# 64-key remainder of a sigmoid attention in 64 by 64 products, placed behind the full chunks, with its pieces of v loaded for six pairs at once

## The chip, the cores and the metric

The kernel runs on one core of one Trainium2 chip. The core has a matrix engine (PE, with its weight loads shown apart as PEld), a vector engine (DVE), a scalar engine (ACT), GpSimd (POOL) and a queue that only issues transfers (SP), and all of them take their instructions in the order of the program. Products land in PSUM, eight banks of 2 KB for each of 128 partitions; everything else is in SBUF. The metric is the device time of one execution in microseconds; lower is better.

## The reference, cut to what matters

Sigmoid attention over 4 batches, 12 heads, 448 positions and 64 channels a head, then two expert layers on the 1792 tokens of 768 channels, all in float32:

```python
def _attn_ref(q, k, v):                       # (4, 12, 448, 64) each
    S = q.shape[2]
    scale = 1.0 / np.sqrt(q.shape[-1])
    scores = scale * np.matmul(q, k.transpose(0, 1, 3, 2)) - np.log(S)
    attn = 1.0 / (1.0 + np.exp(-scores))
    return np.matmul(attn, v).astype(np.float32)

def reference(**kwargs):
    attn_out = _attn_ref(**attn_kwargs)
    x = np.ascontiguousarray(attn_out.transpose(0, 2, 1, 3)).reshape(B * S, H * D)
    x = _moe_ref(x=x, **moe_kwargs)           # h = x @ w_in; (h - tanh(h)) @ w_out, 2048 wide
    return _moe2_ref(x=x, **moe2_kwargs)      # (sigmoid(x @ w_gate) * (x @ w_val)) @ w_out, 1536 wide
```

The weights of the two layers come to the chip as 64-bit floats and are decoded there.

## The kernel before

The 48 heads are taken as 24 pairs (NP); pair p has heads j = 0 and 1, and six pairs (HPB) make a batch. The 448 keys are cut into NCH = 4 chunks of CP = 112. For each pair:

- `load` (L142) brings k and q, with channels on partitions: head j lies on partitions 64j to 64j+63. Each is two transfers of 64 rows, on SP's queue but for the first q. Three buffers each, so pair p+3 is loaded as soon as `split(p)` has read pair p. `load_v` (L155) brings v of a pair in one transfer, keys on 112 partitions.
- `split` (L162) makes of each k and q a rounded high part and a low part (the rest) in fp32r, the faster format of PE: four DVE instructions. The program calls it one pair ahead, and it issues the loads of the pair three ahead.
- `scores` (L191) takes each chunk's transposed scores, keys on partitions, as three products (high by high, low by high, high by low) for each head; contraction is over 64 channels, so the heads use the two halves of the rows of the array. ACT turns them into attention with a sigmoid, into `at`. The two middle chunks use a tile `pa` of two banks and one activation for both heads, the two outer ones a one-bank tile `pb` for each head and two activations. These shapes are the names `sa` and `sb` in the rows below.
- `values` (L226) multiplies with v in plain fp32 (each such product is two instructions in the trace), keys contracted, head j on the column half j of the array and on partitions 64j of the result `pv`, 448 columns wide. ACT copies the result as the high part of x, and DVE subtracts to get the low part.

The program is in the order written by hand (`manual_schedule`, L373), and every engine follows that order; waits between engines are put in by the framework. In the loop over pairs (L395) the order is scores(p), split(p+1), values(p-1). Between them, from pair 3 on, one step at a time of `decode` (L91) for the first seven weight blocks: a (ACT), b and c (DVE; c also fetches a later block), d (ACT and GpSimd), which takes three pairs for a block; `fetch` (L83) issues the transfer of a block of 768 KB on SP, the first two at p = 2 and p = 4. In the last pair, the first expert product `hidden_mm(0)` (L260) and the head of its activations (`hidden_act`, L270: five on ACT, then steps on DVE) come before the values of pair 22, and values(23) follows behind the loop.

After attention the expert layers run as a chain of 80 steps of `hidden_mm` and `project` (L335), in three fp32r products for each block (`mm3`, L246). PSUM: `psa` has two tiles of two banks, `psb` four of one bank (L68, L69).

Of the kernel before, what the change touches and what calls it, by code (L numbers as in the profile page):

```python
# [32 lines left out]
def kernel(  # L33
# [12 lines left out]
    nc = tc.nc  # L46
# [13 lines left out]
    KR = NCH * 128  # L60
# [8 lines left out]
    psb = ctx.enter_context(tc.tile_pool(name="psb", bufs=4, space=bass.MemoryType.PSUM))  # L69
# [72 lines left out]
    def load(p):  # L142

        if p >= NP:
            return
        kt = qkp.tile([128, S], F32, tag="kt", name=f"kt{p}")
        qt = qkp.tile([128, S], F32, tag="qt", name=f"qt{p}")
        for t, src, by in ((kt, k, nc.sync), (qt, q, nc.sync if p else nc.scalar)):

            for j in (0, 1) if by is nc.sync else (1, 0):  # L150
                r = slice(j * D, (j + 1) * D)
                by.dma_start(out=t[r], in_=src[p, r, j])
        qk_t[p] = (qt, kt)

    def load_v(p):  # L155
        if p >= NP:
            return
        vt = atp.tile([CP, 2, NCH, D], F32, tag="vt", name=f"vt{p}")
        nc.sync.dma_start(out=vt, in_=v[p])
        v_t[p] = vt  # L160

    def split(p):  # L162
# [5 lines left out]
        kk = t[:, :2 * KR].rearrange("p (i c r) -> p i c r", i=2, r=128)[:, :, :, :CP]  # L168
        qq = t[:, 2 * KR + QGAP:].rearrange("p (i s) -> p i s", i=2)
        ks = kt.rearrange("p (c r) -> p c r", r=CP)  # L170
        k0 = kk[:, 0].bitcast(F32)
        q0 = qq[:, 0].bitcast(F32)
        if p:
            nc.vector.tensor_copy(out=kk[:, 0], in_=ks)
            nc.vector.tensor_tensor(out=kk[:, 1], in0=ks, in1=k0, op=ALU.subtract)
            nc.vector.tensor_copy(out=qq[:, 0], in_=qt)
            nc.vector.tensor_tensor(out=qq[:, 1], in0=qt, in1=q0, op=ALU.subtract)
        else:

            nc.scalar.activation(out=qq[:, 0], in_=qt, func=AF.Copy)  # L180
            a, b = slice(0, 1), slice(1, NCH)
            nc.vector.tensor_copy(out=kk[:, 0, a], in_=ks[:, a])
            nc.vector.tensor_tensor(out=kk[:, 1, a], in0=ks[:, a], in1=k0[:, a], op=ALU.subtract)
            nc.vector.tensor_copy(out=kk[:, 0, b], in_=ks[:, b])
            nc.vector.tensor_tensor(out=qq[:, 1], in0=qt, in1=q0, op=ALU.subtract)
            nc.vector.tensor_tensor(out=kk[:, 1, b], in0=ks[:, b], in1=k0[:, b], op=ALU.subtract)
        s_t[p] = kk, qq
        load(p + 3)
        load_v(p + 3)

    def scores(p):  # L191

        kk, qq = s_t.pop(p)
        at = atp.tile([CP, 2, NCH, S], F32, tag="at", name=f"at{p}", bufs=2)
        a_t[p] = at

        for c in range(NCH):
            two = 0 < c < NCH - 1
            if two:
                pa = psa.tile([128, 2, 512], F32, tag="pa", name=f"sa{p}_{c}")  # L200
                o = [pa[:CP, j, :S] for j in range(2)]
            else:
                o = []
                for j in range(2):
                    pb = psb.tile([128, 512], F32, tag="pb", name=f"sb{p}_{c}_{j}")
                    o.append(pb[:CP, :S])
            for i, (ki, qi) in enumerate(((0, 0), (1, 0), (0, 1))):
                for j in range(2):
                    r = slice(j * D, (j + 1) * D)
                    nc.tensor.matmul(  # L210
                        o[j], kk[r, ki, c], qq[r, qi],
                        start=(i == 0), stop=(i == 2),
                    )
            if two:
                nc.scalar.activation(  # L215
                    out=at[:, :, c], in_=pa[:CP, :, :S], func=AF.Sigmoid,
                    bias=bias_s[:CP], scale=qk_scale,
                )
            else:
                for j in range(2):  # L220
                    nc.scalar.activation(  # L221
                        out=at[:, j, c], in_=o[j], func=AF.Sigmoid,
                        bias=bias_s[:CP], scale=qk_scale,
                    )

    def values(p):  # L226
        b, hp = divmod(p, HPB)
        at = a_t.pop(p)
        vt = v_t.pop(p)
        po = psb.tile([128, 512], F32, tag="pb", name=f"pv{p}")  # L230
        for c in range(NCH):
            for j in range(2):
                nc.tensor.matmul(  # L233
                    po[j * D:(j + 1) * D, :S], vt[:, j, c], at[:, j, c],
                    start=(c == 0), stop=(c == NCH - 1),
                )
        xh, xl = x[b][:, 0, hp], x[b][:, 1, hp]
        nc.scalar.activation(out=xh, in_=po[:, :S], func=AF.Copy)
        nc.vector.tensor_tensor(out=xl, in0=po[:, :S], in1=xh.bitcast(F32), op=ALU.subtract)
# [133 lines left out]
    with tc.manual_schedule():  # L373
# [8 lines left out]
        load_v(0)  # L382
        load(2)
        load_v(1)
# [4 lines left out]
        pz = psb.tile([128, 512], F32, tag="pb", name="pz")  # L389
# [5 lines left out]
        for p in range(NP):  # L395
# [10 lines left out]
            if p == NP - 1:  # L406
                qk_ctx.close()
# [10 lines left out]
            if p:  # L418
                values(p - 1)
            if len(todo) in (2, 3):  # L420
                todo.pop(0)()
# [3 lines left out]
        values(NP - 1)  # L425
        att_ctx.close()
        ap_ = ctx.enter_context(tc.tile_pool(name="ap", bufs=NB, reuse_waits="tile"))
# [87 lines left out]
```

## Time and profile before

| | |
|---|---|
| Median of 3 runs | 1132.23 us (1132.17 to 1132.34) |
| Profiled execution | 1133.54 us, its span 1131.7 us |
| PE busy | 1124.8 us (99% of the span), 5869 products |
| PEld busy | 994.1 us (88%) |
| DVE busy | 774.6 us (68%) |
| ACT busy | 461.9 us (41%) |
| POOL busy | 215.2 us (19%) |
| Granted clock of PE | 0.999 of 2.4 GHz |
| DMA | 76.44 MB in 24068 packets, mean 68 GB/s |

The profile is of one execution, from its first to its last instruction; the span is that stretch, and the execution's own time has what lies around it. A page gives busy times of each engine, the chain of work that ended last, and groups of instructions; the trace behind it can be asked for an instruction's start, its length and what it waited for. A PE instruction's length is the time until its result is out, so one that follows the other without a gap still overlaps it; what it costs is the distance of two starts. The clock is near full in every slice. Attention takes the first 154 us, the expert layers the rest.

### The profile page before, as it was taken

How to read it: one execution, taken by the hardware profiler on the slowest of the kernel's cores; microseconds unless marked ns; L12 is line 12 of the kernel's file. 1: busy time of each engine (PE TensorE's matmuls, PEld its weight loads, DVE VectorE, ACT ScalarE, POOL GpSimd, SP SyncE). 2: the span in 40 equal slices, each digit the busy share in tenths (PEclk: the TensorE clock that was granted, in tenths of full speed). 3: DMA queues.
4: the chain of work that ended last, by engine and by line, in shares of the span. 5: the costliest groups of instructions: out<-in, count | busy, mean ns of one | idle time of the engine just before them, and what ended most of it. 6: DMA issues, size and time to landing. Idle time of an engine off the chain costs nothing.

```text
span 1131.7 us, 14544 instructions
## 1 busy us (share of the span) xinstructions
PE 1124.8 (99%) x5869; PEld 994.1 (88%) x5869; DVE 774.6 (68%) x1118; ACT 461.9 (41%) x619; POOL 215.2 (19%) x144
## 2 busy tenths in 40 slices
PE   9999999999999999999999999999999999999998
PEld 5555589999999999999999999999999999999997
DVE  3666556888888888888897755656656655665643
ACT  7888844455554444444454321221212212222110
POOL 0011000111111111111128612312312222222210
PEclk9999999999999999999999999999999999999999
DMA  6655300111111111111110211210211201201014
GB/s 192 178 178 159 105 29 1 56 57 56 56 56 56 56 57 56 55 49 51 52 48 28 84 56 35 78 56 29 84 36 49 84 29 56 80 33 56 28 45 152
DMA packets 24068, 76.44 MB, mean 68 GB/s; under 512 B 3392, under 2 KB 12608, under 8 KB 24000
## 3 DMA queue, kind: packets, MB, share of 16 engines
q1 hardware_dynamic: 23840, 75.28, 20.4%
q8 instruction: 46, 0.75, 0.3%
q10 hardware_dynamic: 160, 0.23, 0.1%
q14 instruction: 22, 0.18, 0.1%
HBM read 69.99 MB, written 5.51 MB: 67 GB/s over the span
## 4 chain that ended last, share of the span: by engine, by line
PE 99%; DVE 1%; ACT 0%; issue 0%; ACTq 0%
PE ph L248 17%; PE ph L247 17%; PE ph L249 17%; PE po L248 12%; PE po L247 12%; PE po L249 12%; PE pv L233 7%; PE sb L210 3%; PE sa L210 3%; DVE acc L349 1%; PE pz L391 0%; ACT at L221 0%; ACT at L215 0%; DVE y L282 0%; DVE z L388 0%
## 5 line engine op out<-in xcount | busy, mean ns | idle before, releaser
L349 DVE TENSOR_TENSOR acc<-po,acc 128x448 f32<-128x448 f32 x432 | 251.5, 616 | 249.3 <-PE po L249 249.3
L247 PE MATMUL ph<-x,w 128*128 128x448 f32 x960 | 348.2, 363 | 0.4 <-ACT at L215 0.4
L248 PE MATMUL ph<-x,w 128*128 128x448 f32 x960 | 348.4, 363 | 0.0
L249 PE MATMUL ph<-x,w 128*128 128x448 f32 x960 | 345.6, 360 | 0.0
L128 POOL TENSOR_TENSOR w<-m,w 128x768 fp32r<-128x768 f32 x68 | 126.0, 1852 | 733.7 <-ACT w L127 721.3
L248 PE MATMUL po<-g,w 128*128 128x448 f32 x672 | 244.0, 363 | 0.0
L247 PE MATMUL po<-g,w 128*128 128x448 f32 x672 | 243.6, 362 | 0.0
L249 PE MATMUL po<-g,w 128*128 128x448 f32 x672 | 241.9, 360 | 0.0
L247 PEld LDWEIGHTS ph<-x,w 128*128 128x128 f32 x960 | 180.2, 188 | 15.4 <-ACT at L215 0.8
L249 PEld LDWEIGHTS ph<-x,w 128*128 128x128 f32 x960 | 179.5, 187 | 12.7
L248 PEld LDWEIGHTS ph<-x,w 128*128 128x128 f32 x960 | 180.2, 188 | 9.5
L279 ACT ACTIVATE sg<-ph 128x448 f32<-128x448 f32 x48 | 26.2, 545 | 337.4 <-PE ph L249 337.4
L247 PEld LDWEIGHTS po<-g,w 128*128 128x128 f32 x672 | 126.2, 188 | 9.8
L249 PEld LDWEIGHTS po<-g,w 128*128 128x128 f32 x672 | 125.7, 187 | 8.9
L248 PEld LDWEIGHTS po<-g,w 128*128 128x128 f32 x672 | 126.1, 188 | 6.9 <-POOL g L284 0.3
L101 ACT ACTIVATE m<-st 128x768 f32<-128x768 f32 x68 | 61.8, 908 | 101.4 <-POOL w L128 100.3
L284 POOL TENSOR_TENSOR g<-y,g 128x448 fp32r<-128x448 f32 x48 | 57.3, 1193 | 166.6 <-ACT g L283 128.5
L300 ACT ACTIVATE u<-ph 128x896 f32<-128x896 f32 x32 | 29.4, 918 | 121.0 <-PE ph L249 121.0
L233 PE MATMUL pv<-at,vt 112*64 112x448 f32 x384 | 77.2, 545 | 0.0
L117 DVE SCALAR_TENSOR_TENSOR m<-st,m 128x768 int32<-128x768 int32 x68 | 67.6, 995 | 2.4
L113 DVE SCALAR_TENSOR_TENSOR m<-st,m 128x768 int32<-128x768 int32 x68 | 67.5, 993 | 1.1
L233 PEld LDWEIGHTS pv<-at,vt 112*64 112x64 f32 x384 | 25.5, 136 | 41.3 <-issue 40.7
(48 smaller groups left out, 967.6 us busy)
## 6 DMA issues: line engine op xcount, KB each, us to landing
st<-in_w_out_dram SPq DMA_DIRECT2D x28, 768.0 KB, 4.4
st<-in_w_in_dram SPq DMA_DIRECT2D x16, 768.0 KB, 4.3
st<-in_w_gate_dram SPq DMA_DIRECT2D x12, 768.0 KB, 4.4
st<-in_w_val_dram SPq DMA_DIRECT2D x12, 768.0 KB, 4.2
kt<-in_k_dram SPq DMA_DIRECT2D x48, 112.0 KB, 3.6
vt<-in_v_dram SPq DMA_DIRECT2D x24, 224.0 KB, 2.8
out_dram<-acc SPq DMA_DIRECT2D x24, 224.0 KB, 2.3
qt<-in_q_dram SPq DMA_DIRECT2D x46, 112.0 KB, 3.2
```

Of the source, the lines that this page charges most:

```text
L101: nc.scalar.activation(out=mf, in_=hi.bitcast(F32), func=AF.Abs)
L113: nc.vector.scalar_tensor_tensor(out=m, in0=hi, scalar=-0x40000000, in1=m, op0=ALU.bitwise_and, op1=ALU.bitwise_or,)
L117: nc.vector.scalar_tensor_tensor(out=m, in0=lo, scalar=29, in1=m, op0=ALU.logical_shift_right, op1=ALU.bitwise_or,)
L128: nc.gpsimd.tensor_tensor(out=w1, in0=mf, in1=w0.bitcast(F32), op=ALU.subtract)
L210: nc.tensor.matmul(o[j], kk[r, ki, c], qq[r, qi], start=(i == 0), stop=(i == 2),)
L233: nc.tensor.matmul(po[j * D:(j + 1) * D, :S], vt[:, j, c], at[:, j, c], start=(c == 0), stop=(c == NCH - 1),)
L247: nc.tensor.matmul(o, wt[(slice(None), 0) + wsl], r[(slice(None), 0) + rsl], start=first, stop=False)
L248: nc.tensor.matmul(o, wt[(slice(None), 0) + wsl], r[(slice(None), 1) + rsl], start=False, stop=False)
L249: nc.tensor.matmul(o, wt[(slice(None), 1) + wsl], r[(slice(None), 0) + rsl], start=False, stop=last)
L284: nc.gpsimd.tensor_tensor(out=gt[:, 1, 0], in0=y, in1=gt[:, 0, 0].bitcast(F32), op=ALU.subtract)
L300: nc.scalar.activation(out=uu, in_=h, func=AF.Square)
L349: nc.vector.tensor_tensor(out=at[:, d], in0=po[:, :S], in1=at[:, d], op=ALU.add)
```

## The change

The keys are now cut in three full chunks of 128 and 64 keys left over (KL). The host still hands over v in four chunks of 112 rows, so the kernel puts the chunks of 128 together: 112 rows from the chunk itself and 16 (EX) from the fourth; the last 64 rows of the fourth are the ones left over.

- Loads: k and q get four buffers. v gets one tile for six pairs (VG), two buffers. A pair's three chunks still come pair by pair (now runs of 768 bytes), and the fourth chunk's rows come as ten small transfers for six pairs at once: for each head two copies of the 64 rows left over (on partitions 0 to 63 and on 64 to 127), and three of 16 rows. All their runs are 256 bytes. Those of the first six pairs are issued five before and five behind `load(2)`, later ones three for each `split`.
- `split` works on k in two parts (112 of each chunk's rows and the 16), and leaves the 64 keys alone.
- `scores` takes three chunks, each into two banks with one activation for both heads. The banks are handed out in turn from `psa` (two tiles) and a new `psx` (one tile `px`).
- `scores_last` takes the 64 keys straight from k and q in plain fp32: for each head and each half of 224 positions (SH), a product of 64 channels by 64 keys, on its own quarter of the array, with one activation of 448 columns for all.
- `values` takes the full chunks in two halves of 224 positions, into `pv`, which has one buffer of two banks. `values_last` adds the 64 keys' part, again one quarter of the array for each head and half, and then come the copy and the subtraction as before.
- The order in a pair is scores(p), split(p+1), values(p-1), scores_last(p), values_last(p-1). In the last pair scores_last comes ahead of `hidden_mm(0)`. `psb` is opened behind attention, in the banks of `psx`.

```diff
--- before.py
+++ after.py
@@ -57,7 +57,11 @@
     N1 = G1 * NB
     N2 = F2 * NB
     NSTEP = N1 + N2
-    KR = NCH * 128
+    KR = (NCH - 1) * 128
+    KL = S - KR
+    EX = 128 - CP
+    VG = HPB
+    SH = S // 2
     qk_scale = 1.0 / math.sqrt(D)
     qk_bias = -math.log(S)
@@ -66,7 +70,9 @@
     stp = ctx.enter_context(tc.tile_pool(name="stp", bufs=2))
     dp = ctx.enter_context(tc.tile_pool(name="dp", bufs=1))
     psa = ctx.enter_context(tc.tile_pool(name="psa", bufs=2, space=bass.MemoryType.PSUM))
-    psb = ctx.enter_context(tc.tile_pool(name="psb", bufs=4, space=bass.MemoryType.PSUM))
+    psx_ctx = ExitStack()
+    psx = psx_ctx.enter_context(tc.tile_pool(name="psx", bufs=1, space=bass.MemoryType.PSUM))
     x = [xp.tile([128, 2, KD, S], F32R, tag=f"x{b}", name=f"x{b}") for b in range(NB)]
@@ -143,8 +149,8 @@
         if p >= NP:
             return
-        kt = qkp.tile([128, S], F32, tag="kt", name=f"kt{p}")
-        qt = qkp.tile([128, S], F32, tag="qt", name=f"qt{p}")
+        kt = qkp.tile([128, S], F32, tag="kt", name=f"kt{p}", bufs=4)
+        qt = qkp.tile([128, S], F32, tag="qt", name=f"qt{p}", bufs=4)
         for t, src, by in ((kt, k, nc.sync), (qt, q, nc.sync if p else nc.scalar)):
             for j in (0, 1) if by is nc.sync else (1, 0):
@@ -153,11 +159,38 @@
         qk_t[p] = (qt, kt)
     def load_v(p):
         if p >= NP:
             return
-        vt = atp.tile([CP, 2, NCH, D], F32, tag="vt", name=f"vt{p}")
-        nc.sync.dma_start(out=vt, in_=v[p])
-        v_t[p] = vt
+        g, n = divmod(p, VG)
+        if n == 0:
+            v_t[g] = atp.tile([128, VG, 2, NCH, D], F32, tag="vt", name=f"vt{g}", bufs=2)
+            rest_of(g)
+        nc.sync.dma_start(out=v_t[g][:CP, n, :, :NCH - 1], in_=v[p, :, :, :NCH - 1])
+    pieces = []
+    def rest_of(g):
+        vt = v_t[g]
+        ps = slice(g * VG, (g + 1) * VG)
+        for j in range(2):
+            for h in range(2):
+                pieces.append((
+                    vt[h * KL:(h + 1) * KL, :, j, NCH - 1],
+                    v[ps, CP - KL:, j, NCH - 1].rearrange("n r d -> r n d"),
+                ))
+            for c in range(NCH - 1):
+                pieces.append((
+                    vt[CP:, :, j, c],
+                    v[ps, c * EX:(c + 1) * EX, j, NCH - 1].rearrange("n r d -> r n d"),
+                ))
+    def load_pieces(n):
+        for _ in range(min(n, len(pieces))):
+            o, i = pieces.pop(0)
+            nc.sync.dma_start(out=o, in_=i)
     def split(p):
@@ -165,78 +198,104 @@
             return
         qt, kt = qk_t.pop(p)
         t = qkp.tile([128, 2 * KR + QGAP + 2 * S], F32R, tag="sp", name=f"sp{p}", bufs=2)
-        kk = t[:, :2 * KR].rearrange("p (i c r) -> p i c r", i=2, r=128)[:, :, :, :CP]
+        kk = t[:, :2 * KR].rearrange("p (i c r) -> p i c r", i=2, r=128)
         qq = t[:, 2 * KR + QGAP:].rearrange("p (i s) -> p i s", i=2)
-        ks = kt.rearrange("p (c r) -> p c r", r=CP)
-        k0 = kk[:, 0].bitcast(F32)
-        q0 = qq[:, 0].bitcast(F32)
+        parts = (
+            (kt[:, :KR - (NCH - 1) * EX].rearrange("p (c r) -> p c r", r=CP), slice(0, CP)),
+            (kt[:, (NCH - 1) * CP:KR].rearrange("p (c r) -> p c r", r=EX), slice(CP, 128)),
+        )
+        for src, r in parts:
+            nc.vector.tensor_copy(out=kk[:, 0, :, r], in_=src)
+        if p == 0:
+            nc.scalar.activation(out=qq[:, 0], in_=qt, func=AF.Copy)
+        for src, r in parts:
+            nc.vector.tensor_tensor(
+                out=kk[:, 1, :, r], in0=src, in1=kk[:, 0, :, r].bitcast(F32), op=ALU.subtract
+            )
         if p:
-            nc.vector.tensor_copy(out=kk[:, 0], in_=ks)
-            nc.vector.tensor_tensor(out=kk[:, 1], in0=ks, in1=k0, op=ALU.subtract)
             nc.vector.tensor_copy(out=qq[:, 0], in_=qt)
-            nc.vector.tensor_tensor(out=qq[:, 1], in0=qt, in1=q0, op=ALU.subtract)
...
+        nc.vector.tensor_tensor(out=qq[:, 1], in0=qt, in1=qq[:, 0].bitcast(F32), op=ALU.subtract)
+        s_t[p] = kk, qq, kt, qt
         load(p + 3)
         load_v(p + 3)
+        load_pieces(3)
+    slots = [0]
+    l_t = {}
+    o_t = {}
+    def slot(name):
+        n = slots[0]
+        slots[0] += 1
+        if n % 3 < 2:
+            return psa.tile([128, 2, 512], F32, tag="pa", name=name)
+        return psx.tile([128, 2, 512], F32, tag="px", name=name)
     def scores(p):
-        kk, qq = s_t.pop(p)
...
+        kk, qq, kt, qt = s_t.pop(p)
+        at = atp.tile([128, 2, NCH - 1, S], F32, tag="at", name=f"at{p}", bufs=2)
+        al = atp.tile([128, 2, SH], F32, tag="al", name=f"al{p}", bufs=2)
+        a_t[p] = at, al
+        l_t[p] = kt, qt, al
+        for c in range(NCH - 1):
+            pa = slot(f"sa{p}_{c}")
+            for i, (ki, qi) in enumerate(((0, 0), (0, 1), (1, 0))):
                 for j in range(2):
                     r = slice(j * D, (j + 1) * D)
                     nc.tensor.matmul(
-                        o[j], kk[r, ki, c], qq[r, qi],
+                        pa[:, j, :S], kk[r, ki, c], qq[r, qi],
                         start=(i == 0), stop=(i == 2),
                     )
-            if two:
-                nc.scalar.activation(
-                    out=at[:, :, c], in_=pa[:CP, :, :S], func=AF.Sigmoid,
-                    bias=bias_s[:CP], scale=qk_scale,
+            nc.scalar.activation(
+                out=at[:, :, c], in_=pa[:, :, :S], func=AF.Sigmoid,
+                bias=bias_s, scale=qk_scale,
+            )
+    def scores_last(p):
+        kt, qt, al = l_t.pop(p)
+        pl = slot(f"sl{p}")
+        for h in range(2):
+            for j in range(2):
+                r = slice(j * D, (j + 1) * D)
+                nc.tensor.matmul(
+                    pl[h * KL:(h + 1) * KL, j, :SH], kt[r, KR:], qt[r, h * SH:(h + 1) * SH],
+                    start=True, stop=True,
                 )
-            else:
+        nc.scalar.activation(
+            out=al, in_=pl[:, :, :SH], func=AF.Sigmoid, bias=bias_s, scale=qk_scale
+        )
+    def values(p):
+        at, al = a_t.pop(p)
+        g, n = divmod(p, VG)
+        vt = v_t[g]
+        po = psx.tile([128, 2, 512], F32, tag="pv", name=f"pv{p}")
+        for h in range(2):
+            for c in range(NCH - 1):
                 for j in range(2):
-                    nc.scalar.activation(
-                        out=at[:, j, c], in_=o[j], func=AF.Sigmoid,
-                        bias=bias_s[:CP], scale=qk_scale,
+                    nc.tensor.matmul(
+                        po[j * D:(j + 1) * D, h, :SH], vt[:, n, j, c],
+                        at[:, j, c, h * SH:(h + 1) * SH],
+                        start=(c == 0), stop=False,
                     )
-    def values(p):
+        o_t[p] = po, al, vt, n
+    def values_last(p):
         b, hp = divmod(p, HPB)
-        at = a_t.pop(p)
-        vt = v_t.pop(p)
-        po = psb.tile([128, 512], F32, tag="pb", name=f"pv{p}")
-        for c in range(NCH):
+        po, al, vt, n = o_t.pop(p)
+        for h in range(2):
+            r = slice(h * KL, (h + 1) * KL)
             for j in range(2):
                 nc.tensor.matmul(
-                    po[j * D:(j + 1) * D, :S], vt[:, j, c], at[:, j, c],
-                    start=(c == 0), stop=(c == NCH - 1),
+                    po[j * D:(j + 1) * D, h, :SH], vt[r, n, j, NCH - 1], al[r, j],
+                    start=False, stop=True,
                 )
-        xh, xl = x[b][:, 0, hp], x[b][:, 1, hp]
-        nc.scalar.activation(out=xh, in_=po[:, :S], func=AF.Copy)
-        nc.vector.tensor_tensor(out=xl, in0=po[:, :S], in1=xh.bitcast(F32), op=ALU.subtract)
+        xh, xl = (x[b][:, i, hp].rearrange("p (h s) -> p h s", h=2) for i in range(2))
+        nc.scalar.activation(out=xh, in_=po[:, :, :SH], func=AF.Copy)
+        nc.vector.tensor_tensor(out=xl, in0=po[:, :, :SH], in1=xh.bitcast(F32), op=ALU.subtract)
     h_t = {}
     g_t = {}
@@ -380,13 +439,15 @@
         nc.scalar.activation(out=gb[:, 3:4], in_=bias_s, func=AF.Sigmoid)
         load(1)
         load_v(0)
+        load_pieces(5)
         load(2)
+        load_pieces(5)
         load_v(1)
         load_v(2)
         z = xp.tile([128, S], mybir.dt.bfloat16, tag="z", name="z")
         nc.vector.memset(z, 0.0)
-        pz = psb.tile([128, 512], F32, tag="pb", name="pz")
+        pz = psx.tile([128, 512], F32, tag="pv", name="pz")
         for _ in range(13):
             nc.tensor.matmul(pz[:, :S], z[:, :128], z, start=True, stop=True)
         split(0)
@@ -404,6 +465,7 @@
                 todo.pop(0)()
             split(p + 1)
             if p == NP - 1:
+                scores_last(p)
                 qk_ctx.close()
                 gp = ctx.enter_context(
                     tc.tile_pool(name="gp", bufs=2, side="right", reuse_waits="tile")
@@ -417,13 +479,22 @@
                     f()
             if p:
                 values(p - 1)
+            if p < NP - 1:
+                scores_last(p)
+            if p:
+                values_last(p - 1)
             if len(todo) in (2, 3):
                 todo.pop(0)()
         assert not todo
         for f in extra[3:]:
             f()
         values(NP - 1)
+        values_last(NP - 1)
         att_ctx.close()
+        psx_ctx.close()
+        psb = ctx.enter_context(
+            tc.tile_pool(name="psb", bufs=4, space=bass.MemoryType.PSUM, reuse_waits="tile")
+        )
         ap_ = ctx.enter_context(tc.tile_pool(name="ap", bufs=NB, reuse_waits="tile"))
         rest = []
         for i in range(NSTEP):
```

## Rows read from the trace of the kernel before

**Rows 1.** The chain that ended last: shares of the span by engine and line.

```profile
PE 99%; DVE 1%; ACT 0%; issue 0%; ACTq 0%
PE ph L248 17%; PE ph L247 17%; PE ph L249 17%; PE po L248 12%; PE po L247 12%; PE po L249 12%; PE pv L233 7%; PE sb L210 3%; PE sa L210 3%; DVE acc L349 1%; PE pz L391 0%; ACT at L221 0%; ACT at L215 0%; DVE y L282 0%; DVE z L388 0%
```

**Rows 2.** Timeline of one pair: start and length in us, engine, line, operation, count, [idle before].

```profile
85.28 0.86 PE L210 MATMUL sb<-sp 64*112 64x448 f32 x6
...
85.40 0.55 ACT L238 ACTIVATE x<-pv 128x448 fp32r<-128x448 f32 x1 [1.01 <-PE pv L233]
...
85.98 1.39 PE L210 MATMUL sa<-sp 64*112 64x448 f32 x12
...
87.20 0.77 PE L210 MATMUL sb<-sp 64*112 64x448 f32 x6
87.28 1.91 ACT L215 ACTIVATE at<-sa,bias_s 112x896 f32<-112x896 f32 x2
87.50 0.96 DVE L117 SCALAR_TENSOR_TENSOR m<-st,m 128x768 int32<-128x768 int32 x1
...
87.90 3.23 PE L233 MATMUL pv<-at,vt 112*64 112x448 f32 x16
88.33 0.14 PEld L233 LDWEIGHTS pv<-at,vt 112*64 112x64 f32 x2 [0.23 <-issue]
...
89.76 0.63 DVE L177 TENSOR_TENSOR sp<-qt,sp 128x448 fp32r<-128x448 f32 x1
...
91.06 0.87 PE L210 MATMUL sb<-sp 64*112 64x448 f32 x6
```

**Rows 3.** Groups of instructions, first 250 us: count | busy us, mean ns | idle before.

```profile
L210 PE MATMUL sa<-sp 64*112 64x448 f32 x288 | 33.6, 363 | 0.0
...
L210 PEld LDWEIGHTS sa<-sp 64*112 64x112 f32 x288 | 25.3, 171 | 4.2 <-ACT at L215 0.4
...
L248 PEld LDWEIGHTS ph<-x,w 128*128 128x128 f32 x96 | 18.0, 188 | 0.9
```

**Rows 4.** Stretch of attention: length, busy us (count) by engine, clock, DMA share, GB/s.

```profile
60.00:90.00 30.00, 30.00 (x208) 15.90 (x206) 18.21 (x34) 26.16 (x41) 1.85 (x1) 1.00 0.55 163
```

**Rows 5.** Groups, as rows 3: parts of the first pair's keys on DVE.

```profile
L186 DVE TENSOR_TENSOR sp<-kt,sp 128x336 fp32r<-128x336 f32 x1 | 0.5, 501 | 0.0
...
L183 DVE TENSOR_TENSOR sp<-kt,sp 128x112 fp32r<-128x112 f32 x1 | 0.3, 276 | 0.0
```

**Rows 6.** Timeline of the start; then tile vt: issue ns min/median/max, landing.

```profile
0.74 2.48 SPq L152 DMA_DIRECT2D kt<-in_k_dram  x4
...
4.54 0.58 SPq L159 DMA_DIRECT2D vt<-in_v_dram  x1
...
15.40 0.86 PE L210 MATMUL sb<-sp 64*112 64x448 f32 x6
...
L159 SPq DMA_DIRECT2D vt<-in_v_dram x24: 317/318/582, 4.5 to 125.9; - x24
...
DMA to landing us min/median/max: 2.6/2.8/4.5
```

**Rows 7.** Timeline: the first weights' fetch and use; then landing of tile st.

```profile
21.66 0.42 SPq L88 DMA_DIRECT2D st<-in_w_in_dram  x1
...
27.20 0.89 ACT L101 ACTIVATE m<-st 128x768 f32<-128x768 f32 x1 [1.06 <-DMA st<-in_w_in_dram]
...
DMA to landing us min/median/max: 4.8/6.6/7.8
```

**Rows 8.** Timeline of the end of attention.

```profile
140.44 0.47 PE L247 MATMUL ph<-x,w 128*128 128x448 f32 x1 [0.37 <-ACT at L215]
...
147.85 6.23 PE L233 MATMUL pv<-at,vt 112*64 112x448 f32 x32
...
153.08 0.62 DVE L239 TENSOR_TENSOR x<-pv,x 128x448 fp32r<-128x448 f32 x1
```

**Rows 9.** DMA queue, first 28 us: packets, MB, share of 16 engines.

```profile
q1 hardware_dynamic: 2992, 5.15, 63.1%
```

More of the change, by code (lines that the diff above doesn't have):

```diff
@@ L176, in split @@
             nc.vector.tensor_copy(out=qq[:, 0], in_=qt)
-            nc.vector.tensor_tensor(out=qq[:, 1], in0=qt, in1=q0, op=ALU.subtract)
-        else:
[L180 to L186, printed above, removed]
@@ L187, in split @@
-        s_t[p] = kk, qq
+        nc.vector.tensor_tensor(out=qq[:, 1], in0=qt, in1=qq[:, 0].bitcast(F32), op=ALU.subtract)
+        s_t[p] = kk, qq, kt, qt
         load(p + 3)
         load_v(p + 3)
-    def scores(p):
-        kk, qq = s_t.pop(p)
-        at = atp.tile([CP, 2, NCH, S], F32, tag="at", name=f"at{p}", bufs=2)
-        a_t[p] = at
-        for c in range(NCH):
-            two = 0 < c < NCH - 1
-            if two:
[L200 to L207, printed above, removed]
+        load_pieces(3)
@@ L210, in scores @@
                     nc.tensor.matmul(
-                        o[j], kk[r, ki, c], qq[r, qi],
+                        pa[:, j, :S], kk[r, ki, c], qq[r, qi],
                         start=(i == 0), stop=(i == 2),
                     )
-            if two:
-                nc.scalar.activation(
-                    out=at[:, :, c], in_=pa[:CP, :, :S], func=AF.Sigmoid,
-                    bias=bias_s[:CP], scale=qk_scale,
-                )
-            else:
+            nc.scalar.activation(
+                out=at[:, :, c], in_=pa[:, :, :S], func=AF.Sigmoid,
+                bias=bias_s, scale=qk_scale,
+            )
@@ L227, in values @@
+    def values_last(p):
         b, hp = divmod(p, HPB)
-        at = a_t.pop(p)
-        vt = v_t.pop(p)
-        po = psb.tile([128, 512], F32, tag="pb", name=f"pv{p}")
-        for c in range(NCH):
+        po, al, vt, n = o_t.pop(p)
+        for h in range(2):
+            r = slice(h * KL, (h + 1) * KL)
             for j in range(2):
                 nc.tensor.matmul(
-                    po[j * D:(j + 1) * D, :S], vt[:, j, c], at[:, j, c],
-                    start=(c == 0), stop=(c == NCH - 1),
-                )
```

## Prediction

> **What bounds the kernel now.** I read the chain of waits first: it is PE for 99% of the span [rows 1]. So the time is what PE issues, plus any wait that comes to stand in front of it. The reader sees there that 87% of the chain is the two expert layers (ph and po), which the change leaves alone, and 13% is attention (pv, sb, sa).
>
> Second view, the timeline of one steady pair, from the start of its scores at 85.28 us to the next one's at 91.06 [rows 2]: 5.78 us, PE without a gap. Scores take 2.62 us (85.28 to 87.90), values 3.16 (87.90 to 91.06). Inside, the twelve `sa` instructions take 1.22 us (85.98 to 87.20). The two heads sit on different row halves and run side by side: six steps of 0.203 us, although one instruction lasts 363 ns [rows 3]. The values are sixteen instructions, two for each product; the weight loads come in twos, 0.14 us of load after 0.23 of idleness, so eight steps of 0.375 us with two instructions side by side on the two column halves. What is left are the turns from one array layout to the other: 2.62 - 12 x 0.203 = 0.18 us with the scores, 3.16 - 8 x 0.375 = 0.16 with the values.
>
> Third, the busy times of a stretch of attention: in 30 us ACT works 26.2 and DVE 18.2 [rows 4]. Both have room, ACT not much.
>
> **The change on PE, pair by pair.** Scores: three chunks in place of four, so 9 x 0.203 = 1.83 us, and 0.18 for the turns. A chunk has 128 keys instead of 112, so its weight loads get longer (171 ns now; 188 for the 128 columns of the expert layers [rows 3]) and still fit under a step. Bounds of a step: the 0.188 of half a value step to 0.22 (the load's 17 ns added in full), or -0.1 to +0.15 us a pair; I keep 0.203.
>
> Values, full chunks: 3 chunks x 2 halves x 2 heads x 2 instructions = 24, each with half the columns: 12 steps of 0.188 = 2.26, and 0.16 for the turns. The load is done 0.14 us into a step, so it still fits. Bounds: 0.188, or 0.203 if a step never gets shorter than a score's (+0.2 us); I take the first, since a step of values shows nothing but its columns' time.
>
> Products of 64 by 64: eight instructions in scores_last, eight in values_last, 224 columns each, 0.188 us each. No row shows four quarters of the array at once. Rows show two row halves at once and two column halves at once; the row halves write to different banks, and the change keeps that (bank j in scores_last, bank h in values_last). Four at once: 2 + 2 steps = 0.75 us. Two at once: 1.50. I take 0.75, because each of the two ways of sharing is in the trace and neither uses the other's half, and keep 1.50 as the other end. One more turn: 0.15.
>
> The page "TensorEngine Tiling (Array Packing)" of the Trainium skill, section Tiling Modes, lists 64x64 as four independent tiles; by it the products cost 0.75 us, while this trace alone allows anything up to 1.50.
>
> Sum: 1.83 + 0.18 + 2.26 + 0.16 + 0.75 + 0.15 = 5.33 against 5.78: 0.45 us a pair. From scores(2) to scores(23) there are 21 such periods: **-9.5 us**. The last pair's scores before the first hidden product, with a wait of 0.37 for ACT [rows 8]: 2.62 + 0.37 now, 2.01 + 0.37 + 0.15 + 0.3 after: **-0.2**.
>
> **What hides under it.** ACT: three activations of 0.955 (1.91 for two) and two of 0.55 are 4.0 us a pair, the decoding's two in every third pair (0.95 and less) 0.6: 4.6 of 5.33. No cost; without this cover ACT would set the period. DVE: keys are now split in 336 and 48 columns; pieces of 336 take 0.50, of 112 0.28 [rows 5], the two instructions on q at most 0.63 each, so split is 2.8 us at most. The worst place is a pair behind decode's step c (two of 0.96): subtraction done 1.4 us into the period, c at 3.3, split at 6.1 at most. The first products want all but its last 0.63: 5.5 at most against 5.33. Cost 0 to 0.2 in seven pairs. kt's buffer now comes free only at scores_last(p-1), 4.9 us into a period; four issues of 0.64 us and a landing of up to 4.5 [rows 6] are over 4 us ahead of split(p+3). The tenth piece of a group goes out in the pair before the one that wants it, and is in about 1 us ahead. For all this **+0.4**.
>
> **The start: a wait that is added.** Values(0) now starts 3.16 ahead of 15.40, at 12.24. SP issues one transfer after another at 0.64 us (four kt from 0.74 to 3.22, v0 from 4.54 for 0.58) [rows 6]. Behind v0 now come five pieces, load(2)'s four, five more pieces: the first piece of head 1 that values(0) reads (the 8th) is the 12th transfer behind v0, at 4.54 + 12 x 0.64 = 12.2, and lands 2.8 later (median of v): 15.0, with a margin 15.4. Everything behind it on PE waits: scores_last(1), values_last(0), scores(2). Then 2.4 and 1.0 us of PE: scores(2) at 18.8 instead of 15.40: **+3.4**. If pieces go out at 0.32 (the median of a v, on a quiet queue), the 8th lands at 13: +0.8. If each takes twice 0.64: +8.
>
> **The first weights.** SP's queue is ten issues longer: fetch(0), at 21.66 now, becomes the 38th, at 0.74 + 38 x 0.64 = 25. Its data let ACT go on at 27.20, 5.5 us later, after 1.06 of waiting that PE did not feel [rows 7]. Now that is 30.5, while pair 3's activations (scores at 24.1) are through at 27.8. Queued behind on ACT are scores_last(3)'s activation and the copy of values 2: decode to 31.4, activation 31.9, copy 32.5, DVE's subtraction 33.1. values(3) wants that only pv bank at 31.5: **+1.7** on PE, between 0 and 4 by landings of 4.8 to 7.8 [rows 7].
>
> **The end: one pv bank instead of four.** Now 32 value instructions run through in 6.2 us behind hidden_mm(0), from 147.85. The copy of values 22 stands on ACT behind five activations of the hidden layer, its subtraction on DVE behind three steps: 153.08 to 153.70, 5.85 us after the hidden product [rows 8]. With one buffer for pv, values(23) must wait for that. PE: values(22) with its rest is done after 2.9, waits to 5.9, then 2.4 + 0.6: 8.9 instead of 6.2: **+2.7**, between 2.5 and 3.
>
> Sum: -9.5 - 0.2 + 0.4 + 3.4 + 1.7 + 2.7 = **-1.5 us** on the profiled execution's 1133.54 (span 1131.7). That one lies 1.3 us over the median of the runs; taken off the median: 1132.23 - 1.5 = **1130.7 us**. The clock was granted in full in that stretch [rows 4], without a wait of 3 us on PE; if the two new ones let it fall to 1.2 GHz, each microsecond at that level gives back half of one: 2 or 3 more at most.
>
> **Rivals.**
> - *The quarters run two at a time* (the other side). Place: scores_last and values_last, on PE in every pair. For it: the trace has no case of four, and the two instructions of one product stand in a row in the queue. Against it: halves of both kinds overlap in full. Price 0.75 x 23 = 17 us: **1148**. It turns the sign once the products cost over 0.81 us a pair. Chance 0.15.
> - *Pieces go out fast*: the start costs 0.8, the first weights 0.3. Then -5.5: **1126.7**. For it: a median of 0.32 for v. Against it: at the start issues without a wait took 0.6. Chance 0.22.
> - *Runs of 256 bytes cost as much as long ones.* In the first 28 us a packet took 0.631 x 28 x 16 / 2992 = 94 ns on average, at 1.7 KB [rows 9]. A group of six pairs brings 2 x (2 x 64 + 3 x 16) x 6 = 2112 runs of 256 bytes: by bytes 1.9 us of all sixteen queues, at 94 ns 12.4. The latter puts values(0) at about 20 us, 5 later than in my sum, and later fills queues that stand at 55% [rows 4] with 39% more, in a shorter period, so that pairs wait now and then: 5 to 11 us, **1139**. Chance 0.11.
>
> The page "DMA: Bandwidth & Descriptors" of the Trainium skill, section Specifications, wants 512 bytes a transfer for full rate: it speaks for this last rival. No run here has such pieces.
>
> **How the numbers follow.** Likeliest, with all three waits: 1130.7, chance 0.52, its own range 1127 to 1135. About 2.3 us (0.2%) is what can be told from no change, so faster means under 1130.0. Of the 0.52 I put 0.20 faster, 0.28 within, 0.04 slower. Faster 0.20 + 0.22 = 0.42; same 0.28; slower 0.04 + 0.11 + 0.15 = 0.30. Range 1123 to 1147: the fast case with its spread, the costly runs, a part of the two-at-a-time case.
>
> **What would show it.** A period of 5.3 us between score starts with PE unbroken, scores_last and values_last together some 0.9 us with their turn (1.65 would be the first rival). A gap on PE before values(0) to about 15 us, released by a DMA of vt. ACT idle before decode's first step for 2 us or more in pair 3, and PE then waiting for an activation or DVE's subtraction. A PE gap of 3 us before the last values. I am wrong if ACT or DVE sets the period, if the 64-by-64 products do not overlap, or if values(6), (12) or (18) wait for pieces.

## The result, and the profile after

The changed kernel takes 1142.88 us (median of 4 runs, 1141.89 to 1143.75); the kernel before, in the same comparison, 1132.26. The ratio is 1.0092, 95% interval 1.008 to 1.0104: slower by about 10.6 us, where 1.5 us less was forecast. The profiled execution took 1142.09 us with a span of 1140.3, 8.6 more than the span before. (It lies 0.8 us below its median and the profiled one of before 1.3 above, so 2 us of the 10.6 stand in no trace.)

The page of the changed kernel, its busy times and the chain by engine: PE is still the bound, but no longer without gaps: it has 92% of the chain where it had 99% [rows 1], DVE 3% where it had 1%, and SP's queue and a DMA 1% each.

```profile
PE 1119.7 (98%) x6301; PEld 1011.6 (89%) x6301; DVE 783.5 (69%) x1164; ACT 446.1 (39%) x571; POOL 215.3 (19%) x144
...
PE 92%; DVE 3%; SPq 1%; ACT 1%; DMA 1%; issue 1%; ACTq 0%
```

The two timelines laid side by side give where the 8.6 us are. "Forecast" is the term of the prediction's sum.

| stretch | before | after | forecast | measured |
|---|---|---|---|---|
| to the start of scores(2) | 15.40 | 19.61 | +3.4 | +4.2 |
| 21 periods at the steady length (5.35) | 121.97 | 112.4 | -9.5 | -9.6 |
| pairs longer than that (DVE late; 0.2 of it a late piece of v) | | 8.8 | +0.4 | +8.8 |
| first weights | | 0.5 | +1.7 | +0.5 |
| last pair's scores | 3.07 | 2.94 | -0.2 | -0.1 |
| last two pairs' values | 6.16 | 10.55 | +2.7 | +4.4 |
| the rest | 977.69 | 978.14 | 0 | +0.4 |

The first hidden product, 7.41 us in both, is left out. The 121.97 of before hold 0.4 us that its own first weights cost PE: the pair from 26.98 took 6.20 us where the others take 5.79, since its last `sb` products lasted 1.19 us and not 0.78 (timeline of the kernel before). So the shorter period by itself saves 9.2 us, not 9.6.

```profile
28.90 1.19 PE L210 MATMUL sb<-sp 64*112 64x448 f32 x6
```

Timeline of the changed kernel, a pair with a hold (an operation of DVE that GpSimd makes wait) and the one behind it (columns as in [rows 2]). The pair that starts at 76.66 has its first two products, then PE stands for 1.17 us until DVE's last operation of split is done. That operation (L217) lasts 2.12 us here, and 0.62 in the next pair (80.19); GpSimd's subtraction of decode runs from 75.90 to 77.76.

```profile
75.90 1.86 POOL L134 TENSOR_TENSOR w<-m,w 128x768 fp32r<-128x768 f32 x1 [15.62 <-ACT w L133]
...
76.13 2.12 DVE L217 TENSOR_TENSOR sp<-qt,sp 128x448 fp32r<-128x448 f32 x1
...
76.66 0.47 PE L248 MATMUL sa<-sp 64*128 64x448 f32 x2
...
78.30 1.88 PE L248 MATMUL sa<-sp 64*128 64x448 f32 x16 [1.17 <-DVE sp L217]
...
80.19 0.62 DVE L217 TENSOR_TENSOR sp<-qt,sp 128x448 fp32r<-128x448 f32 x1
...
82.53 0.61 PE L263 MATMUL sl<-qt,kt 64*64 64x224 f32 x8
...
82.96 0.56 PE L292 MATMUL pv<-al,vt 64*64 64x224 f32 x8
...
83.45 0.88 PE L248 MATMUL sa<-sp 64*128 64x448 f32 x6
```

Six pairs are like it (starting at 41.49, 59.17, 76.66, 94.15, 111.64, 129.12): 6.79 us each instead of 5.35, 6 x 1.44 = 8.6 us, nearly the whole of the unforeseen term. (Of the 1.44, 1.17 is PE standing; the rest is that the first two products, 0.47 us long, have nothing behind them to overlap.) The waits of the whole trace (total, times, longest) say the same, a seventh being in the first pair's split:

```profile
PE sa L248 <- DVE sp L217: 7.5, 7, 1.2
PE pv L279 <- DVE x L298: 3.1, 2, 2.9
PE pv L279 <- DMA vt<-in_v_dram: 2.1, 1, 2.1
```

The same fence shows the change's own work: the sixteen products of 64 by 64 take 83.45 - 82.53 = 0.92 us, turn included.

Timelines of the start and of the end of attention:

```profile
11.92 0.59 PE L279 MATMUL pv<-at,vt 128*64 128x224 f32 x2
14.60 4.17 PE L279 MATMUL pv<-at,vt 128*64 128x224 f32 x22 [2.09 <-DMA vt<-in_v_dram]
...
19.61 2.08 PE L248 MATMUL sa<-sp 64*128 64x448 f32 x18
21.63 2.49 PE L279 MATMUL pv<-at,vt 128*64 128x224 f32 x24
...
154.03 0.61 PE L292 MATMUL pv<-al,vt 64*64 64x224 f32 x8
157.52 4.18 PE L279 MATMUL pv<-at,vt 128*64 128x224 f32 x24 [2.88 <-DVE x L298]
```

Both waits are where the prediction put them (values(0) for a piece of v, the last values for the single bank). Behind both, products of which 24 take 2.49 us elsewhere take 4.2 (22 of them at the start, 24 at the end). The stretches say why (columns as in [rows 4]): the granted clock is at half, the 1.2 GHz level.

```profile
16.00:18.00 2.00, 2.00 (x14) 1.27 (x11) 0.00 (x0) 0.00 (x0) 0.00 (x0) 0.50 0.77 226
...
159.00:161.60 2.60, 2.60 (x16) 1.42 (x12) 1.58 (x2) 0.95 (x1) 0.00 (x0) 0.53 0.00 0
```

### The profile page after: what moved, and what is told of

It reads as the page before. It is cut to its first block, busy times and chain, and to the rows that moved or that the text cites. A ratio compares the mean times of both kernels' runs of the same rounds, so it can differ in the third digit from the quotient of the medians.

```text
span 1140.3 us, 15487 instructions
## 1 busy us (share of the span) xinstructions
PE 1119.7 (98%) x6301; PEld 1011.6 (89%) x6301; DVE 783.5 (69%) x1164; ACT 446.1 (39%) x571; POOL 215.3 (19%) x144
## 4 chain that ended last, share of the span: by engine, by line
PE 92%; DVE 3%; SPq 1%; ACT 1%; DMA 1%; issue 1%; ACTq 0%
PE ph L307 17%; PE ph L306 17%; PE ph L308 17%; PE po L307 12%; PE po L306 12%; PE po L308 11%; PE pv L279 4%; PE sa L248 2%; DVE sp L217 1%; SPq L158 1%; PE sl L263 1%; DVE acc L408 1%; DVE x L298 0%; DMA st<-in_w_in_dram 0%; DMA qt<-in_q_dram 0%
## 5 line engine op out<-in xcount | busy, mean ns | idle before, releaser
L252 ACT ACTIVATE at<-sa,bias_s 128x896 f32<-128x896 f32 x72 | 67.3, 1008 | 12.7 <-PE sa L248 11.4
L279 PE MATMUL pv<-at,vt 128*64 128x224 f32 x576 | 63.9, 371 | 5.2 <-DVE x L298 3.1
```

Source lines behind the costliest of these rows:

```text
L252: nc.scalar.activation(out=at[:, :, c], in_=pa[:, :, :S], func=AF.Sigmoid, bias=bias_s, scale=qk_scale,)
L279: nc.tensor.matmul(po[j * D:(j + 1) * D, h, :SH], vt[:, n, j, c], at[:, j, c, h * SH:(h + 1) * SH], start=(c == 0), stop=False,)
```

## The experiments

Times are medians; each ratio is against runs of the kernel before on the same chip.

**e1: decode's last step behind the values.** Step d (ACT's copy, then GpSimd's subtraction) is issued behind values_last, not ahead of split. Split and step c stay as they are.

```diff
-            if len(todo) in (1, 4):
+            if len(todo) == 4:
...
-            if len(todo) in (2, 3):
+            if len(todo) in (1, 2, 3):
```

> Decode's step d (an ACT copy and GpSimd's subtraction) is issued behind values_last instead of ahead of split. Theory: in six pairs GpSimd's subtraction holds DVE's last instruction of split (2.12 us instead of 0.63), and PE's scores wait for it, 1.44 us each time. Then the six waits go, the pairs behind step c take 5.35 us like the others, and the time falls by 8.6 us from 1142.9 to about 1134.3. Rival: DVE's row of subtraction, step c and split is too long by itself for a period of 5.35 us. Then these pairs still wait 1 us or more, and the time stays within 2 us of 1142.9, since c and split stand where they stood.

Measured: 1135.77 us, ratio 1.0025 [1.0015, 1.0034]; 7.1 less than the changed kernel. The six long pairs are gone. GpSimd still holds a DVE operation, but an earlier one, in time for the scores (timeline of e1):

```profile
43.26 0.60 DVE L208 CAST sp<-kt 128x336 fp32r<-128x336 f32 x2
...
43.50 1.83 POOL L134 TENSOR_TENSOR w<-m,w 128x768 fp32r<-128x768 f32 x1 [43.06 <-ACT w L133]
43.79 2.02 DVE L212 TENSOR_TENSOR sp<-kt,sp 128x336 fp32r<-128x336 f32 x2
...
47.14 1.70 PEld L248 LDWEIGHTS sa<-sp 64*128 64x128 f32 x18 [0.33 <-ACT m L107]
...
52.17 1.73 PE L279 MATMUL pv<-at,vt 128*64 128x224 f32 x14 [1.67 <-DMA vt<-in_v_dram]
...
54.75 1.48 PE L248 MATMUL sa<-sp 64*128 64x448 f32 x12
```

So it is not split's length behind step c that is too long; that is unchanged here. The last two lines show a wait that the hold in the pair ahead had covered in part: values(6) wait 1.67 us for the last piece of their group, and that pair takes 7.61 us (47.14 to 54.75), where it took 5.55 in the changed kernel.

**e2: a second bank for the last pair.**

```diff
-        po = psx.tile([128, 2, 512], F32, tag="pv", name=f"pv{p}")
+        po = psx.tile([128, 2, 512], F32, tag="px" if p == NP - 1 else "pv", name=f"pv{p}")
```

> The values of the last pair go to the other two-bank tile (px), which is free by then; all else as in the changed kernel. Theory: the 2.95 us gap before values(23) and the slow clock behind it (4.1 us for 24 instructions that take 2.5) come from the single pv tile alone. Then hidden_mm(1) starts some 5.9 us behind hidden_mm(0)'s end instead of 10.8, and the time falls by 4.5 us to about 1138.4. Rival: PE would wait there anyway, for ACT's or DVE's work on the hidden layer. Then the gap moves to the next product, and the time falls by less than 1.5 us.

Measured: 1139.4 us, ratio 1.0058 [1.0041, 1.0075]. The end runs through in 5.9 us at full clock, 4.6 less, as expected (timeline of e2); part of it was lost elsewhere: the pair of the first weights (from 29.07) took 9.47 us, against 5.82 in the changed kernel's profile, and the start gave back only 1.2 of that.

```profile
153.81 2.49 PE L279 MATMUL pv<-at,vt 128*64 128x224 f32 x24
156.23 0.61 PE L292 MATMUL pv<-al,vt 64*64 64x224 f32 x8
156.76 2.49 PE L279 MATMUL pv<-at,vt 128*64 128x224 f32 x24
159.19 0.61 PE L292 MATMUL pv<-al,vt 64*64 64x224 f32 x8
```

**e3: the first group's pieces in the order of their use**, three of them on ACT's queue.

```diff
...
+        pieces[:] = [pieces[n] for n in (2, 3, 4, 7, 8, 9, 0, 1, 5, 6)]
-        load_pieces(5)
+        load_pieces(3)
         load(2)
-        load_pieces(5)
+        first = pieces[:3]
+        del pieces[:3]
+        load_pieces(4)
...
         split(0)
+        for o, i in first:
+            nc.scalar.dma_start(out=o, in_=i)
```

> The first ten pieces go out in the order in which they are wanted: three of 16 rows ahead of load(2) on SP, the other head's three on ACT's queue while ACT waits for PE, and the four of 64 rows behind load(2). Theory: the order on SP's queue makes values(0) late, and the wait of 2.1 us makes the clock fall. Then values(0) runs through from about 11.9 us at full clock, scores(2) starts at about 15.3 us instead of 19.6, and the time falls by 4.3 us to about 1138.6. Rival: runs of 256 bytes land late whatever the order. Then values(0) still waits 1 us or more, and less than 2 us are gained.

Measured: 1143.76 us, ratio 1.0098 [1.0083, 1.0113]: a miss. The start gained 3.8 us of the 4.3 expected, scores(2) begin at 15.85. More than that was given back at the first weights (timeline of e3, then the stretch 33 to 36):

```profile
26.55 1.48 PE L248 MATMUL sa<-sp 64*128 64x448 f32 x12
...
31.01 0.89 ACT L107 ACTIVATE m<-st 128x768 f32<-128x768 f32 x1 [6.03 <-DMA st<-in_w_in_dram]
...
32.48 1.49 PE L248 MATMUL sa<-sp 64*128 64x448 f32 x6 [4.45 <-ACT al L267]
...
38.98 1.28 PE L248 MATMUL sa<-sp 64*128 64x448 f32 x10
```

```profile
33.00:36.00 3.00, 3.00 (x18) 1.75 (x16) 2.93 (x9) 2.56 (x3) 0.00 (x0) 0.50 0.67 168
```

PE came to pair 4 sooner, the weights did not: ACT stands behind their fetch, PE behind ACT for 4.45 us, and goes on at half the clock. The pair took 12.43 us.

**e4: the three edits together.**

> The three edits together. If each cost is what its theory says and they do not hide behind one another, 8.6 + 4.5 + 4.3 = 17.4 us go and the time is about 1125.5 us, 6.7 us under the kernel before. By the rivals (a DVE row too long in each period, a wait at the end that only moves) it stays above 1135.

Measured: 1130.85 us, ratio 0.9985 [0.9975, 0.9994], a little under the kernel before and 5 above what was expected. Two waits are left (timeline of e4): ACT for the first weights, 4.40 us, and values(6) for their pieces, 1.90.

```profile
29.04 0.89 ACT L107 ACTIVATE m<-st 128x768 f32<-128x768 f32 x1 [4.40 <-DMA st<-in_w_in_dram]
...
30.50 0.88 PE L248 MATMUL sa<-sp 64*128 64x448 f32 x6 [2.82 <-ACT al L267]
...
50.88 1.73 PE L279 MATMUL pv<-at,vt 128*64 128x224 f32 x14 [1.90 <-DMA vt<-in_v_dram]
```

**e5: e4, with the first two weight fetches one pair earlier.**

```diff
-            if p in (2, 4):
-                fetch(p // 2 - 1)
+            if p in (1, 3):
+                fetch(p // 2)
```

> The three edits of e4 together, and the first two weight fetches put one pair earlier in SP's order (at the start of pairs 1 and 3, not 2 and 4). Theory: in e4 the pair that starts at 26.20 took 8.74 us instead of 5.35 because ScalarE stands in order behind its first weights (idle 4.40 for the fetch's landing at 29.04), and SP issued that fetch only at 23.95, behind the loads of a later pair; a fetch issued some 5 us earlier lands before ScalarE asks: -3.4 us, 1127.5. Rival: the 16 DMA engines are full there (0.94 of 27:30), so the wait only moves to the loads of k, q or v displaced: 1130 to 1131, with a new wait of TensorE or VectorE for a DMA between 20 and 35 us.

Measured: 1132.69 us, ratio 0.9996 [0.9987, 1.0006]: 1.8 us more than e4, and over even the rival's time. ACT's wait did go (0.28 us at 26.47). But other transfers came later: PE waited 1.5 us for v in values_last(0), and 4.12 in values(6), after which the clock was at half until 57 us; that pair took 12.36 us (timeline of e5, then a stretch).

```profile
51.29 3.25 PE L279 MATMUL pv<-at,vt 128*64 128x224 f32 x14 [4.12 <-DMA vt<-in_v_dram]
```

```profile
53.00:57.00 4.00, 4.00 (x30) 2.10 (x28) 0.09 (x1) 1.18 (x2) 0.00 (x0) 0.52 0.05 13
```

**e6: e5, with four pieces behind each split instead of three.**

```diff
-        load_pieces(3)
+        load_pieces(4)
```

> e5, and four pieces of v issued behind each split instead of three, so that a group's ten pieces are out one pair earlier. Theory: the pairs that start at 45.62 and 112.27 in e4 took 7.84 and 6.05 us because their values waited for the last piece of their group (TensorE idle 1.90 for v at 50.88): -2.5 and -0.7, so 1124.3 with e5's gain. Rival: the fourth issue (about 0.6 us on SP) delays the next k and q loads, and the periods of the pairs in which it stands grow: no gain over e5, or a loss of some 1 us.

Measured: 1125.51 us, ratio 0.9937 [0.9922, 0.9952]: 7.0 us under the kernel before, 17 under the changed one, and the fastest of all versions. Every pair but one takes the steady length; that one loses 0.9 us to what is left of the first weights (timeline of e6).

```profile
15.27 2.08 PE L248 MATMUL sa<-sp 64*128 64x448 f32 x18
...
25.98 1.48 PE L248 MATMUL sa<-sp 64*128 64x448 f32 x12
27.83 0.88 PE L248 MATMUL sa<-sp 64*128 64x448 f32 x6 [0.38 <-ACT al L267]
...
32.27 2.08 PE L248 MATMUL sa<-sp 64*128 64x448 f32 x18
```

**e7: the changed kernel with GpSimd's subtraction cut in four.** The direct test of the hold: same place, same work.

```diff
-            nc.gpsimd.tensor_tensor(out=w1, in0=mf, in1=w0.bitcast(F32), op=ALU.subtract)
+            for e in range(4):
+                s = slice(e * WC // 4, (e + 1) * WC // 4)
+                nc.gpsimd.tensor_tensor(
+                    out=w1[:, s], in0=mf[:, s], in1=w0[:, s].bitcast(F32), op=ALU.subtract
+                )
```

> The changed kernel with nothing but GpSimd's subtraction of a decode (768 columns, 1.85 us) cut into four of 192 columns, at the same place. Theory: VectorE's operation on two operands in SBUF is held until the GpSimd instruction that runs beside it ends; with instructions of about 0.5 us it gets in between them, L217 takes 0.7 to 1.2 us instead of 2.12, and each of the six waits of 1.44 us falls to 0.1 to 0.5: 1135.5 to 1138. Rival: the two engines share the reads evenly or GpSimd goes first for as long as it has work queued, so that L217 still takes about 2.1 us and the waits stay: 1142 to 1144.

Measured: 1138.0 us, ratio 1.0049 [1.0034, 1.0064]. GpSimd is busier than before (2.70 us for the four), yet the same operation of DVE (here L221) takes 0.90 us instead of 2.12, and the pair 5.57 instead of 6.79 (timeline of e7):

```profile
75.11 2.70 POOL L136 TENSOR_TENSOR w<-m,w 128x192 fp32r<-128x192 f32 x4 [13.57 <-ACT w L133]
...
75.34 0.90 DVE L221 TENSOR_TENSOR sp<-qt,sp 128x448 fp32r<-128x448 f32 x1
...
75.87 2.30 PE L252 MATMUL sa<-sp 64*128 64x448 f32 x18
...
81.44 2.08 PE L252 MATMUL sa<-sp 64*128 64x448 f32 x18
```

DVE waits for the instruction that runs on GpSimd, and gets in between two of them. Evenly shared reads would have left L221 as long as it was: that rival falls. This agrees with the Trainium skill, page "SBUF — State Buffer", section "SBUF: two separate sides": the port pair of VectorE and GpSimd is locked for a whole instruction, and VectorE needs it when both its inputs are in SBUF. Of the six long pairs' 8.6 us this run took back 6 x 1.22 = 7.3; its median is only 4.9 lower. The profiled execution gained another 1.9 at the start, where a wait of 2.04 us cost no clock (scores(2) at 17.67), but lost 4.3 at the first weights (the pair from 28.37 took 9.64) and 1.8 in the pair from 81.44, which waited for v.

**e8: e1 and e2 together, without e3.**

> The edits of e1 and e2 together, without that of e3 (the order of the first pieces). Theory: the waits for GpSimd (7.1 us, e1) and for the last pair's accumulation bank (4.6 us in its tail, e2) are at different places and add: 1142.9 - 7.1 - 4.6 = 1131.2, and if the wait for the first weights is as long as in e2 (9.47 for that pair, 4.1 above 5.35) 1134 to 1135. Rival: the start's edit is what e4 has to thank for its lead over before (3.8 us at scores of pair 2), so without it the time is 1134.7 whatever the first weights do.

Measured: 1132.34 us, ratio 0.9998 [0.9988, 1.0007], between the theory's two cases: the two gains add, and the pair of the first weights took 9.92 us here.

**e9: e6 without the edit of the start.**

> e6 without the edit of e3: the first group's pieces go out in the changed kernel's order, all on SP. Theory: the start is a cost of its own, as the prediction had it: values of pair 0 wait about 2 us for v, TensorE then runs them at the lower granted clock, and the scores of pair 2 begin near 19.6 instead of 15.27; nothing gives it back, so 1125.5 + 4.3 = 1129.8. Rival: the first transfers are bound by their volume, so that what the start loses is not waited for later (at the first weights or at a piece), as e3 against the changed kernel had it: 1125 to 1127.

Measured: 1127.63 us (1125.79 to 1128.7), ratio 0.9949 [0.9933, 0.9965]. Neither in full. In the profiled execution (1128.7) scores(2) begin at 19.86, 4.6 us behind e6's, values(0) having waited 2.42 us and run on at half the clock; only 0.9 of that comes back, since the first weights now cost nothing. Two of the five executions (1125.79 and 1125.98) come to e6's time; their granted clock over the whole run was 1.000 and 0.999, that of the others 0.997 to 0.998. That suggests that the clock did not fall at their start; no trace of them shows it. The start's order is worth 2.1 us in the median, with executions that overlap (e6: 1124.55 to 1126.06).

**e10: the kernel before with e5's line.**

> The kernel before, with the one line of e5: its first two weight fetches put one pair earlier in SP's order. Theory: the kernel before loses at most what its own first weights cost it (its periods near 27 us are 0.4 us above 5.78), so 1132.1 to 1132.5, and the lead of e6 is of the changed kernel's shorter period (21 times 0.43). Rival: a good part of e6's lead of 7 us is owed to the earlier fetch, which the kernel before would gain from as well: 1127 to 1130.

Measured: 1132.46 us, ratio 0.9999 [0.9989, 1.0009]. The earlier fetch gives the kernel before nothing, so e6's lead is not one that the kernel before could have had from that line. In e6's profile the way from scores(2) to scores(23) takes 113.2 us, 8.7 less than in the kernel before.

## Why the prediction was wrong

It forecast a little faster, and the kernel became slower. The mechanism that it priced is there; one step failed, and a cost named in passing was left out of the sum.

- **"period 5.33 against 5.78": right.** 5.35 us wherever nothing waits. The 64-by-64 products overlap four at a time (0.92 us with the turn, forecast 0.9), so the rival of two at a time falls, and the four independent tiles of the Trainium skill ("TensorEngine Tiling (Array Packing)", Tiling Modes) agree.
- **"What hides under it", "Cost 0 to 0.2 in seven pairs": wrong, the step that failed.** 8.8 us against 0.4, which is 8.4 of the 10.1 us between the forecast (-1.5) and the profiled execution (+8.6). It did not decide the sign alone: e1, without these waits, is still 0.25% over the kernel before. The prediction rightly found the worst pair (step c ahead of split) and that split would end within a few tenths of its time there. But it took each operation of DVE at the length that it has alone (0.63), and asked only what stands ahead of it on DVE. What runs beside it on GpSimd was not asked. By then split is late enough in the period to meet decode's step d: 2.12 us instead of 0.63. e1 (step d moved) and e7 (step d cut) show it from two sides. The trace of before had it, harmless, in a row that the prediction did not read: a cast of 0.39 us that took 0.84 beside GpSimd, in six pairs (timeline of the kernel before):

```profile
91.04 1.84 POOL L128 TENSOR_TENSOR w<-m,w 128x768 fp32r<-128x768 f32 x1 [15.51 <-ACT w L127]
91.76 0.62 DVE L239 TENSOR_TENSOR x<-pv,x 128x448 fp32r<-128x448 f32 x1 [1.37 <-ACT x L238]
92.30 0.84 DVE L174 CAST sp<-kt 128x448 fp32r<-128x448 f32 x1
```

- **"The end: one pv bank": right place and wait (2.88 us), wrong size.** 4.4 against 2.7; the difference is the clock, 4.18 - 2.49 = 1.7. e2 removes all of it.
- **"The start": right wait, size off.** +4.2 against +3.4. The piece came 0.8 us sooner than forecast (14.60 for 15.4), and the clock took 4.17 - 2.49 x 22/24 = 1.9. The prediction said that two such waits might let the clock fall, for "2 or 3 more at most", and left it out of the sum. It was 3.6.
- **"The first weights": +0.5 in the profiled execution against +1.7.** The order of events was right (ACT in order behind the fetch, PE behind ACT; 1.49 us of idleness at ACT). But that it cost so little was luck, and the reading that PE did not feel the wait of before was wrong (0.4, above). In the profiled executions the pair that starts with scores(4) pays what PE arrives ahead of the weights, some 0.55 us on top, and 1.7 to 2.1 more where the clock fell behind the wait:

| | scores(4) start | ACT starts on the weights | that pair beyond 5.35 | clock fell |
|---|---|---|---|---|
| changed kernel | 30.31 | 30.23 | 0.5 | no |
| e1 | 30.42 | 30.55 | 0.7 | no |
| e4 | 26.20 | 29.04 | 3.4 | no |
| e2 | 29.07 | 30.96 | 4.1 | yes |
| e7 | 28.37 | 30.42 | 4.3 | yes |
| e3 | 26.55 | 31.01 | 7.1 | yes |

The changed kernel paid little here because its own late start brought PE there just when the weights landed; what makes the start quicker is paid back at this place until the fetch is moved (e5, e6).
- **Pieces for values(6): "in about 1 us ahead": wrong.** Even in the changed kernel the last piece came a little late: these products take 2.69 us and not 2.49 (timeline of the changed kernel). The hold in the pair ahead hid a part of the wait: e1, e4 and e5, which have no such long pair, wait 1.7 to 4.1 us there.

```profile
50.28 2.69 PE L279 MATMUL pv<-at,vt 128*64 128x224 f32 x24
```

- **"Runs of 256 bytes cost as much as long ones": falls.** The queue in the first 28 us of the changed kernel, to be read beside [rows 9]: nearly twice the packets in less of the engines' time, 0.565 x 28 x 16 / 5537 = 46 ns each against 94. The Trainium skill, page "DMA: Bandwidth & Descriptors", section Specifications, wants 512 bytes for full rate. By the trace's records of the packets, the 2112 of 256 bytes took 18 ns each in the mean and those of 1792 bytes 97, so short ones were a quarter dearer by the byte, which agrees in direction, and far from as dear as a long one each.

```profile
q1 hardware_dynamic: 5537, 4.50, 56.5%
```

Left open: why the clock falls behind one wait and not behind another of the same length, why the first weights landed 5.0 us behind their issue in one execution (changed kernel) and 7.5 in another (e9), and whether the 1.2 us between e6 and its forecast have one cause.

## What to carry to other kernels

Where an edit brings an operation of DVE nearer to its deadline, look up what GpSimd runs at that moment, and count GpSimd's whole instruction; moving or cutting that instruction is the cheap cure. A wait of some 2 to 3 us newly put on PE costs its own length and, in most cases here, 1.7 to 1.9 us more in clock, so price it with both. When one wait is taken away, look which transfer was just in time: in e3 and e5 the gain came back as a longer wait three pairs on, and e6, with the fetches and the pieces early, kept it.

## What was not expected of the hardware

- A wait of PE did not always cost clock. Of the 17 waits of 1.9 us and more in attention in these traces, 13 took the granted clock to 0.50, among them 2.09 and 2.88 us (changed kernel), 2.42 (e9), 4.12 (e5) and 4.45 (e3). Four did not: 2.57 (e2) and 2.04 (e7) at the start, where the changed kernel's 2.09 did, and 2.82 at 30 and 1.90 at 50 in e4. That execution of e4 is the only one of its ten with a granted clock of 1.000 over the whole; the others have 0.995 to 0.999. (Timeline of e2, then stretches of e4, the waits and what follows them.)

```profile
15.04 2.48 PE L279 MATMUL pv<-at,vt 128*64 128x224 f32 x22 [2.57 <-DMA vt<-in_v_dram]
```

```profile
28.00:30.00 2.00, 0.00 (x0) 0.00 (x0) 0.00 (x0) 0.96 (x2) 0.00 (x0) 1.00 0.92 252
30.00:32.00 2.00, 1.28 (x10) 0.83 (x12) 1.08 (x2) 2.00 (x4) 0.00 (x0) 1.00 0.69 152
...
51.00:53.00 2.00, 2.00 (x26) 1.32 (x30) 0.00 (x0) 0.00 (x0) 0.00 (x0) 1.00 0.67 188
```

- DVE's subtraction with one operand in PSUM was not held beside GpSimd (0.62 us at 91.76 in the rows of before above), while a cast of 448 columns with a single input in SBUF was (0.84 at 92.30). The changed kernel's casts of 336 and 48 columns were not: the two take 0.60 us alone (50.74 in the changed kernel), 0.60 at 43.26 in e1, where the second begins while GpSimd runs, and 0.61 at 44.82 in e7, beside the last quarter of GpSimd's work. So the number of inputs alone does not tell which casts are held.
